# Adding up all three passes of a split product in one PSUM bank, and another order for the first operations

## The chip, the cores and the metric

The kernel runs on one core of a Trainium2 chip. The metric is the device time of one execution in microseconds (us), as the median of several runs. Beside it stands a profiled execution, from which all views are taken; its span runs from the first to the last instruction of the program.

Engines: PE is the matrix engine (PEld its weight loads), DVE the vector engine, ACT the scalar engine, POOL the general engine, SP the queue that issues DMAs. PE writes its sums to PSUM, which consists of banks of 512 float32 values for each of 128 partitions; ACT and DVE read them from there.

## The reference

A decayed linear attention over blocks of 64 tokens, then a two-layer network with a leaky ReLU on its output:

```python
q, k, v: (4, 8, 768, 64) float32     lam: (8,) float32
w_in: (512, 2048) float64            w_out: (2048, 512) float64
...
for b in range(nb):
    intra = (qb @ kb.T * Dmask) @ vb
    inter = (qb * lam_pow) @ kv_state
    out[b] = intra + inter
    kv_state = lam_block * kv_state + (kb * rev_pow).T @ vb
x = attn_out as (3072, 512)
h = x @ w_in
g = maximum(0.01 * h, h)
return float32(g @ w_out)
```

The weights come as 64-bit floats. The kernel turns each into float32 with integer and ACT arithmetic on its two words (`to_float32`).

## The kernel before

**Split products.** A float32 product is made from three passes of a faster format (`float32r`). An operand is split into a head `h`, a rest `l` and a combination `m`; a weight likewise into `wh`, `wl`, `wm` (`parts`, line 802). The passes are xh by wh (z = 0), xl by wl (z = 1) and xm by wm (z = 2). The first two have another scale than the third. So the sum of the first two is multiplied by S + 1 (S = 4096) before the third is added to it.

**Stages.** The 3072 tokens are 24 chunks of 128 (`NCH`), in six groups of four (`NG`, `GC`). Three stages overlap:

- *Attention rounds* (`round_of(c)`, one for each chunk). A round loads k, q and v (lines 466, 524), transposes k and q on PE (L546), copies them from PSUM to SBUF on ACT (L527), and makes scores, states and outputs from many small 64x64 products (L410). The output of a chunk arises in the PSUM tile `po`. ACT takes its head `xh` from there (L692), DVE its rest `xl` (L700), and then `xm` (L718). From chunk 4 on, the transposed k of a later chunk uses the upper half of the same tile `po`, and ACT copies it from there.
- *`up(g, p)`*, the first layer for group g and weight part p (of `NP` = 8). For each half of the part it takes a PSUM bank, adds passes 0 and 1 into it (4 products of 512 columns each), scales the bank in place on ACT (L878), adds pass 2, and applies the leaky ReLU on ACT (L881) into a buffer `gs`, which goes to DRAM as `G`.
- *`down(g, p)`*, the second layer. `down_load` brings G back and splits it (L902 on ACT, L903 and L905 on DVE) into a ring of four. For each of four row blocks (`tb`) of 128 tokens, all parts are added up: passes 0 and 1 in one bank, pass 2 in another. After the last part ACT takes the first bank with its scale to `t` (L943), DVE adds the second (L952), and the rows go out (L955). In the last block of all, pass 2 is cut into 384 and 128 columns, so that the first cut can be added while the second is still computed.

**Banks.** `psc` and `po` are PSUM tiles of two banks each; `pt`, `b10`, `b11` and `b2` have one each. In `up` and in the first rounds, blocks take any of the four single ones. In `down` the row blocks have fixed pairs:

```python
acc = [[z[:, i].rearrange("p y t -> p (y t)") for i in range(2)] for z in (psc, po)] + [
    [b1[0], b2], [b1[1], pt.rearrange("p y t -> p (y t)")]]
ACC = [["psc", "psc"], ["po", "po"], ["b10", "b2"], ["b11", "pt"]]
```

So row block 0 has both banks of psc, 1 both of po, 2 has b10 and b2, 3 has b11 and pt, in every group.

**Order.** A planner (`Plan`) records every operation by `add(engine, cost, function, reads, writes)`. A list `ORDER` gives the first operations by number, with the engine that takes each: (8, "ACT") is operation 8, on ACT. A negative number on PE is so many filler transposes (L349), which keep PE running; nine more (`WARM`) stand ahead of the list. What is not listed, the planner orders by costs and due times. Operations are emitted in that order, and each engine works its own in the order of emission. Waits between engines are put in when the program is built, from which tiles an instruction reads and writes. An engine that waits holds up everything behind it in its queue. SP's queue also counts DMAs on eight semaphores in turn.

Of the kernel before, what the change touches and what calls it, by code (L numbers as in the profile page):

```python
# [27 lines left out]
U = 16.0  # L28
WS = S * U

# [211 lines left out]
def kernel(  # L242
# [22 lines left out]
    T = GC * C  # L265
    WARM = 9
    LATER = 2.0
    ORDER = [(3, "DMA"), (4, "DMA"), (-6, "PE"), (6, "PE"), (8, "ACT"), (7, "PE"), (5, "DMA"), (9, "ACT"), (0, "DVE"), (1, "DVE"), (10, "POOL"), (13, "PE"), (2, "DVE"), (11, "DVE"), (15, "DVE"), (12, "PE"), (14, "DVE"), (-1, "PE"), (19, "PE"), (20, "PE"), (16, "POOL"), (17, "DVE"), (21, "DVE"), (101, "DMA"), (26, "DMA"), (29, "PE"), (33, "DVE"), (22, "PE"), (28, "DMA"), (36, "PE"), (18, "POOL"), (38, "DVE"), (39, "POOL"), (103, "ACT"), (23, "ACT"), (24, "DVE"), (27, "DMA"), (31, "ACT"), (102, "ACT"), (30, "PE"), (32, "ACT"), (-1, "PE"), (35, "PE"), (37, "DVE"), (40, "DVE"), (41, "POOL"), (34, "DVE"), (105, "DVE"), (49, "DMA"), (95, "DMA"), (96, "ACT"), (104, "ACT"), (52, "PE"), (56, "DVE"), (42, "PE"), (43, "PE"), (97, "ACT"), (50, "DMA"), (-1, "PE"), (53, "PE"), (98, "ACT"), (54, "ACT"), (55, "ACT"), (44, "DVE"), (25, "DVE"), (106, "DVE"), (99, "DVE"), (51, "DMA"), (-2, "PE"), (59, "PE"), (45, "PE"), (61, "DVE"), (100, "DVE"), (72, "DMA"), (73, "DMA"), (46, "ACT"), (75, "PE"), (107, "ACT"), (58, "PE"), (57, "DVE"), (47, "DVE"), (60, "DVE"), (76, "PE"), (155, "PE"), (74, "DMA"), (179, "DMA"), (78, "ACT"), (62, "POOL"), (79, "POOL"), (108, "DVE"), (63, "DVE"), (77, "ACT"), (173, "DMA"), (80, "DVE"), (48, "DVE"), (65, "PE"), (66, "PE"), (67, "ACT"), (-2, "PE"), (68, "PE"), (156, "PE"), (-1, "PE"), (81, "PE"), (180, "ACT"), (69, "ACT"), (70, "DVE"), (64, "POOL"), (84, "DVE"), (85, "POOL"), (181, "ACT"), (182, "ACT"), (174, "ACT"), (175, "ACT"), (82, "PE"), (83, "DVE"), (157, "PE"), (158, "PE"), (120, "DMA"), (111, "DMA"), (110, "DMA"), (119, "DMA"), (112, "DMA"), (88, "PE"), (89, "PE"), (114, "PE"), (159, "ACT"), (90, "ACT"), (91, "PE"), (176, "ACT"), (92, "ACT"), (183, "DVE"), (109, "DVE"), (160, "PE"), (123, "PE"), (86, "DVE"), (177, "DVE"), (184, "DVE"), (93, "DVE"), (178, "DVE"), (-1, "PE"), (164, "PE"), (113, "PE"), (165, "PE"), (161, "PE"), (217, "DMA"), (211, "DMA"), (136, "DMA"), (117, "DVE"), (116, "ACT"), (125, "ACT"), (115, "ACT"), (128, "PE"), (129, "PE"), (135, "DMA"), (121, "DMA"), (185, "ACT"), (71, "DVE"), (127, "DVE"), (186, "DVE"), (122, "PE"), (219, "ACT"), (124, "ACT"), (162, "ACT"), (166, "PE"), (241, "PE"), (167, "PE"), (242, "PE"), (138, "PE"), (87, "POOL"), (94, "DVE"), (118, "DVE"), (218, "ACT"), (213, "ACT"), (214, "ACT"), (212, "ACT"), (221, "DVE"), (131, "DVE"), (130, "DVE"), (-1, "PE"), (137, "PE"), (139, "PE"), (140, "PE"), (232, "DMA"), (132, "POOL"), (126, "DVE"), (133, "DVE"), (134, "POOL"), (220, "ACT"), (142, "PE"), (143, "PE"), (215, "DVE"), (222, "DVE"), (141, "ACT"), (243, "ACT"), (168, "ACT"), (144, "PE"), (145, "ACT"), (149, "ACT"), (148, "ACT"), (246, "PE"), (247, "PE"), (169, "PE"), (187, "DVE"), (216, "DVE"), (223, "ACT"), (244, "PE"), (170, "PE"), (234, "ACT"), (248, "ACT"), (151, "DVE"), (224, "DVE"), (153, "DVE"), (189, "DMA"), (226, "DMA"), (163, "DMA"), (188, "DMA"), (154, "DMA"), (275, "DMA"), (252, "PE"), (253, "PE"), (171, "ACT"), (233, "ACT"), (228, "ACT"), (227, "ACT"), (235, "ACT"), (249, "PE"), (191, "PE"), (152, "DVE"), (146, "DVE"), (190, "PE"), (150, "POOL"), (225, "DVE"), (229, "ACT"), (236, "DVE"), (230, "DVE"), (231, "DVE"), (192, "PE"), (193, "PE"), (194, "DVE"), (195, "PE"), (196, "PE"), (197, "PE"), (245, "ACT"), (202, "ACT"), (250, "ACT"), (237, "DVE"), (238, "DVE"), (206, "DVE"), (239, "DVE"), (254, "ACT"), (201, "ACT"), (277, "PE"), (320, "DMA"), (322, "ACT"), (288, "ACT"), (198, "ACT"), (321, "ACT"), (257, "PE"), (258, "PE"), (255, "PE"), (172, "DMA"), (326, "DMA"), (327, "ACT"), (204, "DVE"), (324, "DVE"), (207, "POOL"), (208, "DVE"), (203, "POOL"), (328, "ACT"), (259, "ACT"), (323, "ACT"), (330, "DVE"), (205, "DVE"), (199, "DVE"), (325, "DVE"), (329, "ACT"), (331, "DVE"), (332, "DVE"), (333, "DVE"), (268, "PE"), (269, "PE"), (263, "PE"), (256, "ACT"), (260, "PE"), (352, "DMA"), (274, "DMA"), (354, "ACT"), (210, "DMA"), (276, "PE"), (278, "PE"), (279, "PE"), (298, "DMA"), (281, "PE"), (282, "PE"), (355, "ACT"), (280, "ACT"), (261, "ACT"), (283, "PE"), (300, "PE"), (340, "PE"), (264, "PE"), (284, "ACT"), (311, "ACT"), (346, "DMA"), (251, "DMA"), (289, "POOL"), (209, "POOL"), (292, "DVE"), (293, "POOL"), (353, "ACT"), (265, "ACT"), (291, "DVE"), (446, "DVE"), (335, "PE"), (341, "PE"), (287, "ACT"), (348, "ACT"), (336, "PE"), (349, "ACT"), (270, "ACT"), (347, "ACT"), (356, "DVE"), (240, "DVE"), (266, "PE"), (267, "ACT"), (285, "DVE"), (271, "PE"), (272, "ACT"), (337, "ACT"), (296, "DMA"), (297, "DMA"), (299, "PE"), (301, "PE"), (302, "PE"), (303, "ACT"), (262, "DMA"), (411, "DMA"), (405, "DMA"), (294, "DVE"), (463, "DVE"), (334, "DVE"), (471, "DMA"), (458, "DMA"), (477, "DMA"), (455, "DMA"), (350, "DVE"), (357, "DVE"), (304, "PE"), (305, "PE"), (351, "DVE"), (306, "PE"), (338, "PE"), (358, "ACT"), (310, "ACT"), (307, "ACT"), (359, "DVE"), (308, "DVE"), (286, "DVE"), (309, "DVE"), (450, "DMA"), (273, "DMA"), (339, "ACT"), (342, "ACT"), (413, "ACT"), (407, "ACT"), (406, "ACT"), (388, "PE"), (361, "PE"), (343, "PE"), (362, "PE"), (344, "ACT"), (383, "PE"), (384, "PE"), (389, "PE"), (479, "DMA"), (454, "DMA"), (319, "DMA"), (470, "DMA"), (478, "DMA"), (447, "DMA"), (457, "DMA"), (366, "PE"), (367, "PE"), (360, "DVE"), (314, "DVE"), (200, "DVE"), (295, "POOL"), (412, "ACT"), (415, "DVE"), (147, "DVE"), (385, "ACT"), (390, "ACT"), (414, "ACT"), (408, "ACT"), (368, "ACT"), (391, "PE"), (386, "PE"), (369, "PE"), (468, "DMA"), (345, "DMA"), (472, "DMA"), (431, "DMA"), (437, "DMA"), (451, "DMA"), (464, "DMA"), (363, "ACT"), (364, "PE"), (365, "ACT"), (387, "ACT"), (370, "ACT"), (371, "DMA"), (459, "DMA"), (448, "DMA"), (449, "DMA"), (313, "POOL"), (290, "POOL"), (409, "DVE"), (315, "DVE"), (316, "POOL"), (317, "DVE"), (416, "DVE"), (494, "PE"), (495, "PE"), (312, "POOL"), (497, "PE"), (498, "PE"), (496, "DVE"), (499, "PE"), (410, "DVE"), (417, "DVE"), (461, "DMA"), (453, "DMA"), (462, "DMA"), (456, "DMA"), (503, "DVE"), (392, "ACT"), (452, "DMA"), (460, "DMA"), (393, "DMA"), (418, "DVE"), (432, "ACT"), (435, "DVE"), (433, "ACT"), (434, "ACT"), (436, "DVE"), (394, "PE"), (395, "PE"), (396, "ACT"), (439, "ACT"), (399, "PE"), (440, "ACT"), (372, "PE"), (425, "PE"), (373, "PE"), (438, "ACT"), (374, "ACT"), (465, "DMA"), (474, "DMA"), (400, "PE"), (401, "ACT"), (397, "PE"), (426, "PE"), (402, "PE"), (513, "DVE"), (441, "DVE"), (419, "DVE"), (442, "DVE"), (443, "DVE"), (510, "DVE"), (475, "DMA"), (398, "ACT"), (403, "ACT"), (512, "DMA"), (404, "DMA"), (480, "DVE"), (522, "DVE"), (377, "PE"), (375, "PE"), (376, "ACT"), (427, "ACT"), (555, "PE"), (378, "PE"), (379, "ACT"), (476, "DMA"), (469, "DMA"), (420, "PE"), (421, "PE"), (422, "ACT"), (380, "PE"), (556, "PE"), (381, "ACT"), (423, "PE"), (428, "PE"), (444, "DVE"), (467, "DMA"), (529, "DMA"), (473, "DMA"), (525, "DMA"), (561, "DMA"), (445, "DVE")]
    APART = 4
    FIRST_LOADS = ["k0", "q0", "v0", "k1", "q1", "v1", "w10", "k2", "q2", "v2", "w11", "k3", "q3", "v3"]  # L270
    LOW_PE, MIX_PE = set(), set()
# [772 lines left out]
```

## Time and profile before

| | us |
|---|---|
| median of 3 runs | 608.91 (608.42 to 609.12) |
| span of the profiled execution | 606.1 |
| PE busy, of the span | 595.4 |
| PE idle while waiting, all of it before 31 us | 7.5 |
| DVE / ACT / POOL busy | 308.5 / 266.9 / 73.4 |
| attention rounds and `up` on PE | to about 340 |
| `down` on PE | about 340 to 603 |
| last output row lands | 606.1 |

The busy times say that PE sets the time: in the 40 equal slices of the span every one but the first, second and last is at 9 tenths or more. A product of 512 columns starts 0.227 us after the one before (twelve take 2.72 us), though its own row is 389 ns long, because products are pipelined. An idle stretch of ACT or DVE costs nothing while PE has work.

### The profile page before, as it was taken

How to read it: one execution, taken by the hardware profiler on the slowest of the kernel's cores; microseconds unless marked ns; L12 is line 12 of the kernel's file. 1: busy time of each engine (PE TensorE's matmuls, PEld its weight loads, DVE VectorE, ACT ScalarE, POOL GpSimd, SP SyncE). 2: the span in 40 equal slices, each digit the busy share in tenths (PEclk: the TensorE clock that was granted, in tenths of full speed). 3: DMA queues.
4: the chain of work that ended last, by engine and by line, in shares of the span. 5: the costliest groups of instructions: out<-in, count | busy, mean ns of one | idle time of the engine just before them, and what ended most of it. 6: DMA issues, size and time to landing. Idle time of an engine off the chain costs nothing.

```text
span 606.1 us, 12896 instructions
## 1 busy us (share of the span) xinstructions
PE 595.4 (98%) x5381; PEld 494.4 (82%) x5381; DVE 308.5 (51%) x425; ACT 266.9 (44%) x428; POOL 73.4 (12%) x83
## 2 busy tenths in 40 slices
PE   7899999999999999999999999999999999999997
PEld 5688888888888888888788888888888888888886
DVE  5888855334242344243467755455454544635531
ACT  3789865444555556565566432222312313214111
POOL 2232412214132023122000000000000000000000
PEclk9999999999999999999999999999999999999999
DMA  8998957676889878975775833423333333333201
GB/s 194 230 260 226 267 164 215 148 183 153 202 247 216 215 240 191 262 246 176 263 277 213 290 122 115 163 83 143 122 108 135 109 135 113 132 104 122 87 1 69
DMA packets 147754, 105.18 MB, mean 174 GB/s; under 512 B 123632, under 2 KB 124400, under 8 KB 147696
## 3 DMA queue, kind: packets, MB, share of 16 engines
q1 hardware_dynamic: 147408, 104.29, 58.1%
q8 instruction: 42, 0.69, 0.5%
q14 instruction: 16, 0.13, 0.1%
q10 hardware_dynamic: 288, 0.07, 0.0%
HBM read 68.69 MB, written 35.65 MB: 172 GB/s over the span
## 4 chain that ended last, share of the span: by engine, by line
PE 96%; SPq 2%; DMA 1%; issue 0%; DVE 0%; DVEq 0%; ACT 0%
PE b L853 33%; PE b L920 18%; PE pt L853 11%; PE po L920 11%; PE psc L920 11%; PE po L410 4%; PE pt L920 4%; PE psc L410 3%; SPq L466 2%; DMA gs<-in_k_dram 1%; PE b L546 1%; PE po L546 0%; SPq L781 0%; SPq L524 0%; PE pt L546 0%
## 5 line engine op out<-in xcount | busy, mean ns | idle before, releaser
L902 ACT ACTIVATE xh<-att 128x1024 fp32r<-128x1024 f32 x48 | 50.7, 1060 | 148.7 <-PE b L920 140.7
L903 DVE SCALAR_TENSOR_TENSOR xl<-att,xh 128x1024 fp32r<-128x1024 f32 x48 | 58.6, 1222 | 97.7 <-ACT xh L902 97.7
L853 PE MATMUL b<-xm,wm 128*128 128x512 f32 (+1 forms) x292 | 77.6, 391 | 0.0
L853 PE MATMUL b<-xh,wh 128*128 128x512 f32 (+1 forms) x292 | 77.4, 389 | 0.0
L853 PE MATMUL b<-xl,wl 128*128 128x512 f32 (+1 forms) x292 | 77.4, 388 | 0.0
L920 PE MATMUL b<-wh,xh 128*128 128x512 f32 x192 | 74.7, 389 | 0.0
L920 PE MATMUL b<-wl,xl 128*128 128x512 f32 x192 | 74.7, 389 | 0.0
L853 PEld LDWEIGHTS b<-xl,wl 128*128 128x128 f32 x292 | 54.2, 188 | 11.2
L853 PEld LDWEIGHTS b<-xh,wh 128*128 128x128 f32 x292 | 54.0, 188 | 11.1
L853 PEld LDWEIGHTS b<-xm,wm 128*128 128x128 f32 x292 | 53.5, 188 | 11.4 <-ACT b L878 0.3
L905 DVE SCALAR_TENSOR_TENSOR xm<-xl,xh 128x1024 fp32r<-128x1024 f32 x48 | 58.7, 1226 | 4.7
L878 ACT ACTIVATE b<-b 128x512 f32<-128x512 f32 x72 | 42.0, 586 | 34.8 <-PE b L853 34.8
L881 ACT ACTIVATE gs<-b 128x512 f32<-128x512 f32 x72 | 42.6, 597 | 30.3 <-PE b L853 24.3
L920 PEld LDWEIGHTS b<-wl,xl 128*128 128x128 f32 x192 | 36.0, 188 | 7.5
L920 PEld LDWEIGHTS b<-wh,xh 128*128 128x128 f32 x192 | 36.1, 188 | 7.4
L647 POOL TENSOR_TENSOR att<-att 128x256 f32<-128x256 f32 x40 | 30.9, 772 | 86.8 <-DVE att L644 73.9
L637 DVE TENSOR_TENSOR att<-psc,att 128x512 f32<-128x512 f32 x24 | 16.5, 689 | 45.4 <-PE psc L410 45.3
L920 PE MATMUL psc<-wm,xm 128*128 128x512 f32 (+1 forms) x100 | 37.9, 384 | 0.0
L799 DVE TENSOR_SCALAR w<-w 128x512 int32<-128x512 int32 x32 | 14.9, 468 | 44.1 <-ACT w L793 44.0
L920 PE MATMUL psc<-wh,xh 128*128 128x512 f32 x96 | 37.3, 389 | 0.0
L920 PE MATMUL psc<-wl,xl 128*128 128x512 f32 x96 | 37.3, 389 | 0.0
L920 PE MATMUL po<-wh,xh 128*128 128x512 f32 x96 | 37.3, 389 | 0.0
(98 smaller groups left out, 944.4 us busy)
## 6 DMA issues: line engine op xcount, KB each, us to landing
att<-g SPq DMA_DIRECT2D x48, 512.0 KB, 3.2
g<-gs SPq DMA_DIRECT2D x47, 512.0 KB, 3.6
raw<-in_moe_w_in_dram SPq DMA_DIRECT2D x16, 512.0 KB, 5.3
raw<-in_moe_w_out_dram SPq DMA_DIRECT2D x16, 512.0 KB, 4.6
out_dram<-gs SPq DMA_DIRECT2D x23, 256.0 KB, 2.1
att<-in_k_dram SPq DMA_DIRECT2D x44, 128.0 KB, 4.1
att<-in_v_dram SPq DMA_DIRECT2D x22, 256.0 KB, 4.1
wo<-w SPq DMA_DIRECT2D x8, 512.0 KB, 4.9
```

The source lines that it names most:

```text
L410: nc.tensor.matmul(dst[HALF[cols]], lhsT=lhsT[HALF[rows]], rhs=rhs[HALF[rows]], start=start, stop=True, skip_group_check=True)
L466: nc.sync.dma_start(out=dst[:, z * HP:(z + 1) * HP, :], in_=y[z::2].rearrange("h p d -> p h d"))
L637: add("DVE", 0.685, lambda: nc.vector.tensor_tensor(sc, psc[:, :, lower, :], decay, op=ALU.mult), ["psc", "fk"], ["sc"])
L647: add("POOL", 0.62, lambda new=new, j=j: nc.gpsimd.tensor_tensor(state[(j + 1) % 4], new, _bc(lam_c, 2, D), op=ALU.mult), [f"st{j % 4}", " ...
L799: add("DVE", 0.42, lambda: nc.vector.tensor_scalar(d, d, 3, None, op0=ALU.logical_shift_left), [], [key], lock=True)
L853: nc.tensor.matmul(dst, lhsT=w[z][:, kk * 2 * P + f * P:kk * 2 * P + (f + 1) * P], rhs=x[z][:, kk, toks], start=start and kk == 0, stop=kk ...
L878: add("ACT", ns, lambda b=b: nc.scalar.activation(out=b(), in_=b(), func=AF.Copy, bias=0.0, scale=S + 1.0), [], [kb], rank=-1.5)
L881: add("ACT", ns, lambda b=b, r=r: nc.scalar.activation(out=r(), in_=b(), func=AF.Prelu, bias=0.0, scale=1.0 / WS, alpha=0.01), [kb], [kg], ...
L902: add("ACT", 1.05, lambda: nc.scalar.activation(out=h, in_=graw[j], func=AF.Copy, bias=0.0, scale=NEAR), reads, wr("h"))
L903: add("DVE", 1.215, lambda: nc.vector.scalar_tensor_tensor(l, graw[j], 1.0, h.bitcast(F32), op0=ALU.mult, op1=ALU.subtract), reads + [f"rh ...
L905: add("DVE", 1.215, lambda: nc.vector.scalar_tensor_tensor(m, l.bitcast(F32), -S, h.bitcast(F32), op0=ALU.mult, op1=ALU.add), [f"rh{j}", f ...
L920: nc.tensor.matmul((to if z == 2 else acc[tb][0])[:, cols], lhsT=ring[j][z][:, f * T + tb * P:f * T + (tb + 1) * P], rhs=W[pp][z][:, f * d ...
```

## The change

**`up`.** All three passes of a half add up in one bank with no scaling between; the leaky ReLU follows with scale 1.

```diff
             for i, f in enumerate(fs):
                 add("PE", us, lambda f=f, b=b, i=i: product(b()[:, i, :], f, 0, i == 0), keys("h"), [kb], kind="u")
                 add("PE", us, lambda f=f, b=b, i=i: product(b()[:, i, :], f, 1), keys("l"), [kb], kind="u")
             ns = 0.6 if len(fs) * n == T else 0.4
-            add("ACT", ns, lambda b=b: nc.scalar.activation(out=b(), in_=b(), func=AF.Copy, bias=0.0, scale=S + 1.0), [], [kb], rank=-1.5)
             for i, f in enumerate(fs):
                 add("PE", us, lambda f=f, b=b, i=i: product(b()[:, i, :], f, 2), keys("m"), [kb], kind="u")
-            add("ACT", ns, lambda b=b, r=r: nc.scalar.activation(out=r(), in_=b(), func=AF.Prelu, bias=0.0, scale=1.0 / WS, alpha=0.01),
+            add("ACT", ns, lambda b=b, r=r: nc.scalar.activation(out=r(), in_=b(), func=AF.Prelu, bias=0.0, scale=1.0, alpha=0.01),
                 [kb], [kg], rank=-1.5)
```

**Weight parts.** For that, the scale goes into the second part: the head is a plain copy, `wm` = w - wh, and `wl` = (S + 1) wm + wh. The order of `wl` and `wm` is exchanged. The conversion's scale changes from 2^-110 to 2^-112.

```diff
-                nc.scalar.activation(out=wh, in_=src, func=AF.Copy, bias=0.0, scale=NEAR / S)
+                nc.scalar.copy(wh, src)
...
-        add("DVE", 1.215, lambda: nc.vector.scalar_tensor_tensor(wl, wh.bitcast(F32), -S, src, op0=ALU.mult, op1=ALU.add),
-            keys + [f"wh{p}"], [f"wl{p}"], lock=True)
-        difference(p)
...
+        add("DVE", 1.215, lambda: nc.vector.scalar_tensor_tensor(wm, wh.bitcast(F32), -1.0, src, op0=ALU.mult, op1=ALU.add),
+            keys + [f"wh{p}"], [f"wm{p}"], lock=True)
+        add("DVE", 1.215, lambda: nc.vector.scalar_tensor_tensor(wl, wm.bitcast(F32), S + 1.0, wh.bitcast(F32), op0=ALU.mult, op1=ALU.add),
+            [f"wh{p}", f"wm{p}"], [f"wl{p}"], lock=True)
```

**`down`.** A row block has one bank. The eight banks make two sets: row blocks of even groups use psc's two banks and po's two, those of odd groups use b10, b2, b11 and pt. The planner knows the halves of psc and po by names of their own. A finished block is copied by ACT straight into the output buffer, with no `t` and no sum on DVE. Only the last block of all keeps `t` and the two sums; its third pass goes to two banks of the other set, the halves of psc.

```diff
-    acc = [[z[:, i].rearrange("p y t -> p (y t)") for i in range(2)] for z in (psc, po)] + [
-        [b1[0], b2], [b1[1], pt.rearrange("p y t -> p (y t)")]]
-    ACC = [["psc", "psc"], ["po", "po"], ["b10", "b2"], ["b11", "pt"]]
+    acc = [z[:, i].rearrange("p y t -> p (y t)") for z in (psc, po) for i in range(2)] + [b1[0], b2, b1[1], bank["pt"]]
+    ACC = ["psc0", "psc1", "po0", "po1", "b10", "b2", "b11", "pt"]
...
+            at = g % 2 * GC + tb
...
+            spare = [(1 - g % 2) * GC + i for i in range(2)]
...
+                if not very_last:
+                    add("ACT", 0.6, lambda y=y, at=at: nc.scalar.copy(y, acc[at]), [ACC[at]], [f"gs{jt}"], rank=-1.5)
+                    add("DMA", 0.8, lambda rows=rows, y=y: nc.sync.dma_start(out=rows, in_=y), [f"gs{jt}"], [], rank=-1.5)
+                    continue
...
-                        lambda t=t, y=y, to=to, cols=cols: nc.vector.scalar_tensor_tensor(
-                            y[:, cols], to[:, cols], 1.0 / WS, t[:, cols], op0=ALU.mult, op1=ALU.add),
+                        lambda t=t, y=y, to=to, cols=cols: nc.vector.tensor_tensor(y[:, cols], acc[to][:, cols], t[:, cols], op=ALU.add),
```

**`ORDER`.** The list is another one: 364 operations and 6 fillers where it had 491 and 16. Operations are renumbered, since `up` records fewer. It begins with one half of weight part 1 (95), then q and k of chunk 0 (4, 3), k of chunk 1 (26), v of chunk 0 (5), q of chunk 1 (27), the other half (101) and v of chunk 1 (28). Before, it began with k, q and v of chunk 0 (3, 4, 5), the half 101, then k, v and q of chunk 1 (26, 28, 27), k of chunk 2 (49) and the half 95. Each k and each q is two DMAs, so half 101 was the sixth load. In round 7 of the new list the head `xh` of the output is operation 276, the rest `xl` 277, and the copy of kT for chunk 9 is 279. On ACT and DVE the list has, from the one to the other:

```python
(276, "ACT"), (321, "ACT"), (284, "DVE"), (198, "DVE"), (316, "DVE"), (317, "DVE"), (255, "ACT"),
(279, "ACT"), (283, "DVE"), (322, "DVE"), (323, "DVE"), (324, "DVE"), (277, "DVE")
```

More of the change, by code (lines that the diff above doesn't have):

```diff
@@ L27 @@
 NEAR = 1.0 - 2.0 ** -13
-U = 16.0
-WS = S * U
 def _bc(ap, idx, n):
@@ L355 @@
     kinds = {"bank": list(bank), "raw": [f"raw{i}" for i in range(NRAW)], "low": ["low0", "low1"], "gs": ["gs0", "gs1"]}
-    also = {"gs0": ["gs00", "gs01", "k@2", "v@2"], "gs1": ["gs10", "gs11", "k@3", "v@3"], f"raw{NRAW - 1}": [f"raw{NRAW - 1}", "q@3"]}
+    also = {"gs0": ["gs00", "gs01", "k@2", "v@2"], "gs1": ["gs10", "gs11", "k@3", "v@3"], f"raw{NRAW - 1}": [f"raw{NRAW - 1}", "q@3"], "psc": ["psc0", "psc1"], "po": ["po0", "po1"]}
     early = [Slot("gs", 0), Slot("gs", 1), Slot("raw", NRAW - 1)]
@@ L792, in to_float32 @@
         move(1.6, get, after, [kr], name=f"w{p}{h}" if kind == "wi" else None)
-        add("ACT", 0.66, lambda: nc.scalar.activation(out=dst, in_=words(1, F32), func=AF.Abs, scale=2.0 ** -110),
+        add("ACT", 0.66, lambda: nc.scalar.activation(out=dst, in_=words(1, F32), func=AF.Abs, scale=2.0 ** -112),
             [kr], [key])
@@ L919, in go @@
                         for z in zs:
-                            nc.tensor.matmul((to if z == 2 else acc[tb][0])[:, cols], lhsT=ring[j][z][:, f * T + tb * P:f * T + (tb + 1) * P],
+                            nc.tensor.matmul(to[:, cols], lhsT=ring[j][z][:, f * T + tb * P:f * T + (tb + 1) * P],
                                              rhs=W[pp][z][:, f * d_model:(f + 1) * d_model][:, cols],
-                                             start=pp == 0 and f == 0 and z != 1, stop=pp == NP - 1 and f == 1,
+                                             start=fresh and pp == pps[0] and f == 0 and z == zs[0], stop=pp == NP - 1 and f == 1,
                                              skip_group_check=True)
@@ L930, in down @@
             cut = [slice(0, 3 * P), slice(3 * P, d_model)]
-            ends = [(acc[tb][1], ACC[tb][1]), (acc[0][1], ACC[0][1])]
+            spare = [(1 - g % 2) * GC + i for i in range(2)]
             one, two = (p,), (p + 1,)
-            order = [(one, (0, 1, 2), every), (two, (0, 1, 2), every)]
+            order = [(one, (0, 1, 2), every, at), (two, (0, 1, 2), every, at)]
             if very_last:
-                order = [(one + two, (0, 1), every)] + [(one + two, (2,), x) for x in cut]
-            for pps, zs, cols in order:
-                to, key = ends[cut.index(cols)] if cols in cut else (acc[tb][1], ACC[tb][1])
-                add("PE", 0.227 * 2 * len(pps) * len(zs) * (cols.stop - cols.start) / d_model, lambda pps=pps, zs=zs, cols=cols, to=to, go=go: go(pps, zs, cols, to),
-                    needs(pps, ["hlm"[z] for z in zs]), sorted({key if z == 2 else ACC[tb][0] for z in zs}))
+                order = [(one + two, (0, 1), every, at)] + [(one + two, (2,), x, y) for x, y in zip(cut, spare)]
+            for pps, zs, cols, to in order:
+                fresh = to in spare or 0 in pps
+                add("PE", 0.227 * 2 * len(pps) * len(zs) * (cols.stop - cols.start) / d_model,
+                    lambda pps=pps, zs=zs, cols=cols, to=to, go=go, fresh=fresh: go(pps, zs, cols, acc[to], fresh),
+                    needs(pps, ["hlm"[z] for z in zs]), [ACC[to]])
             if done:
@@ L942, in down @@
                 t, y = tt[jt], gs[jt][:, 0, :]
-                add("ACT", 0.6, lambda t=t, tb=tb: nc.scalar.activation(out=t, in_=acc[tb][0], func=AF.Copy, bias=0.0, scale=(1.0 + 1.0 / S) / U),
-                    [ACC[tb][0]], [f"t{jt}"], rank=-1.5)
                 rows = out[(g * GC + tb) * P:(g * GC + tb + 1) * P, :]
-                for i, cols in enumerate(cut if very_last else [every]):
+                if not very_last:
+                    add("ACT", 0.6, lambda y=y, at=at: nc.scalar.copy(y, acc[at]), [ACC[at]], [f"gs{jt}"], rank=-1.5)
+                    add("DMA", 0.8, lambda rows=rows, y=y: nc.sync.dma_start(out=rows, in_=y), [f"gs{jt}"], [], rank=-1.5)
+                    continue
+                add("ACT", 0.6, lambda t=t, at=at: nc.scalar.copy(t, acc[at]), [ACC[at]], [f"t{jt}"], rank=-1.5)
+                for i, cols in enumerate(cut):
                     n = cols.stop - cols.start
-                    to, key = ends[i]
-                    part_of = f"gs{jt}" + (str(i) if very_last else "")
-                    queue = nc.scalar if i else nc.sync
+                    to, part_of, queue = spare[i], f"gs{jt}{i}", nc.scalar if i else nc.sync
                     add("DVE", 0.14 + 0.55 * n / d_model,
-                        lambda t=t, y=y, to=to, cols=cols: nc.vector.scalar_tensor_tensor(
-                            y[:, cols], to[:, cols], 1.0 / WS, t[:, cols], op0=ALU.mult, op1=ALU.add),
-                        [f"t{jt}", key], [part_of], rank=-1.5)
+                        lambda t=t, y=y, to=to, cols=cols: nc.vector.tensor_tensor(y[:, cols], acc[to][:, cols], t[:, cols], op=ALU.add),
+                        [f"t{jt}", ACC[to]], [part_of], rank=-1.5)
                     add("DMA", 0.8 * n / d_model, lambda rows=rows, y=y, cols=cols, queue=queue: queue.dma_start(out=rows[:, cols], in_=y[:, cols]),
```

10 lines of the change are left out of this document (3 added, 7 removed).

## The prediction

> **What bounds the kernel now.** I read the page's busy shares first, then the busy time by stretch, then TensorE's own waits.
>
> ```profile
> PE 595.4 (98%) x5381; PEld 494.4 (82%) x5381; DVE 308.5 (51%) x425; ACT 266.9 (44%) x428; POOL 73.4 (12%) x83
> ...
> PEclk9999999999999999999999999999999999999999
> ```
> ```profile
> 0.00:45.00 45.00, 37.84 (x819) 32.21 (x820) 33.99 (x70) 29.49 (x50) 13.06 (x20) 1.00 0.94 228
> 45.00:340.00 295.00, 294.72 (x3402) 244.44 (x3402) 145.21 (x236) 173.52 (x307) 60.31 (x63) 1.00 0.77 218
> 340.00:602.00 262.00, 262.00 (x1158) 217.06 (x1157) 128.58 (x118) 63.45 (x73) 0.00 (x0) 1.00 0.33 115
> ```
> ```profile
> PE b L349 <- POOL att L352: 1.4, 1, 1.4
> PE b L546 <- DMA gs<-in_k_dram: 1.3, 1, 1.3
> PE b L410 <- DMA att<-in_v_dram: 1.1, 1, 1.1
> ...
> PE psc L410 <- ACT att L527: 0.6, 1, 0.6
> ```
> In the second view the columns are the stretch, its length and the busy time of PE, PEld, DVE, ACT and POOL, then clock, DMA share and GB/s. From 45 to 602 us PE is busy 556.7 of 557.0 us, at full clock. All of PE's waits together are 7.5 us, in the head, while the first loads land. So work that leaves ACT or DVE after 45 us is worth nothing; the change can win only in the head, and it can lose wherever it puts a wait on PE.
>
> **What it removes.** The products stay: six token groups x 8 parts x 48 of 512 columns, 2304 in all at one every 0.227 us (the chain has 12 in 2.72 us), 523 us. The scaling in the middle of each `up` block goes:
> ```profile
> L878 ACT ACTIVATE b<-b 128x512 f32<-128x512 f32 x72 | 42.0, 586 | 34.8 <-PE b L853 34.8
> ...
> L878 ACT ACTIVATE pt<-pt 128x512 f32<-128x512 f32 x24 | 14.0, 583 | 17.9 <-PE pt L853 17.9
> ...
> L943 ACT ACTIVATE raw<-po 128x512 f32<-128x512 f32 x6 | 3.6, 598 | 12.7 <-PE po L920 12.7
> ...
> L527 ACT COPY att<-po 128x512 f32<-128x512 f32 x6 | 3.6, 592 | 1.1 <-PE po L546 0.9
> ```
> That is 56.0 us of ACT, plus 23 additions of 0.69 on DVE (L952) in `down`. All of it but the share in the head lies under a busy PE: 0. The reworked weight parts are as many instructions of the same shapes, so I cost them as the old rows: 0. If these covers went, nothing follows: both engines are under 60% busy there.
>
> **Down banks: +5.6.** Until now the four row blocks of a group used psc, po, the pair b/b2 and the pair b/pt, so a tile that ACT was emptying was not written again until three blocks later. Now blocks 0 and 1 of an even group are the two halves of psc, and 2 and 3 those of po. In the built program the last pair's first product into psc's second half waits for ACT's copy out of the first half, and the same in po: twice a group, groups 0, 2 and 4, six waits. Odd groups use four separate tiles and have none. One wait: the block's last product ends 0.39 after its start (L920's mean is 389 ns), ACT starts 0.03 later (at the end PE finishes po at 597.23, L943 starts at 597.26), the copy takes 0.59 (L527 on po, above), PE restarts 0.05 later (an L527 ending at 14.54 released PE at 14.60). That is 1.06, less the 0.227 that PE would have spent anyway, 0.83. Then a first product whose weights could not be loaded ahead:
> ```profile
> 41.47 1.20 PE L853 MATMUL b<-xh,wh 128*128 128x512 f32 x4
> 42.51 1.08 PE L853 MATMUL b<-xl,wl 128*128 128x512 f32 x4
> ```
> The first four after other work take 0.12 more; I use 0.11. 6 x 0.94 = 5.6. Bounds: 4.8 with the shortest copy (557 ns) and no reload; 12 if ACT has each time just begun a ring head of 1.06 (L902). ACT is 24% busy here and took the block 0.03 after PE, so the value is near the lower end.
>
> **Round 7's split: +4.4.** In the new list `xh` of round 7 is (276, "ACT"), `xl` (277, "DVE"), and between them stands (279, "ACT"), the copy of kT for a later round. All three read po. In the built program `xl` waits for that copy, which is eighth after `xh` in ACT's queue: six weight operations (L795, L797, L793) and a block's end (L881) are in between. Start to start, ACT takes less than the durations:
> ```profile
> 64.08 0.80 ACT L795 ACTIVATE low<-raw 128x512 uint16<-128x512 uint32 x1
> 64.73 0.79 ACT L797 ACTIVATE low<-raw 128x512 f16<-128x512 f32 x1
> ...
> 70.16 0.59 ACT L527 COPY att<-po 128x512 f32<-128x512 f32 x1
> 70.64 0.60 ACT L692 ACTIVATE xh<-po 128x512 fp32r<-128x512 f32 x1
> ```
> Here 0.65 for L795; likewise 0.63 for L797, 0.55 for L793 and 0.50 for L881. In the queue: 0.50 for `xh`, then 0.65 + 0.50 + 0.63 + 0.55 + 0.65 + 0.63 + 0.55 = 4.16, then the copy's 0.59: 5.25. Then DVE's 0.68 and two hand-overs of 0.05: 6.0, and 0.25 from the last attention product to `xh`: 6.25. PE has eight products queued ahead, 8 x 0.227 + 0.13 to change over = 1.95. So PE stands 4.3, near 70 us, and 0.11 for weights: 4.4. Before, the copy stood ahead of `xh` (70.16, 70.64), and `xl` came right behind at 71.28. Bounds: 0 if `xl` waited for `xh` alone (ready 1.4 after it starts, under the 1.95); 7.4 if two of the weights' loads, which ACT also waits for in that queue, land 1.5 late. Behind `xl` on DVE stand only `xm` and state sums for the same round.
>
> **Round 11: +1.2.** Group 2's first product follows the attention products of round 11 at once and needs their `xh`: 0.25 + 0.60 + 0.05 = 0.9, and then `xl` (0.68 + 0.1) against four products (0.91) that began late, 0.2, with 0.1 for weights. Before, 24 products of blocks with other operands stood there (139.01 to 145.46). Bounds 0 and 2.
>
> **End: +0.3.** The last block's third pass goes into psc's two halves, not pt and psc, so DVE's first sum waits for the second cut:
> ```profile
> 602.31 0.56 PE L920 MATMUL psc<-wm,xm 128*128 128x128 f32 x4
> 602.56 0.56 DVE L952 SCALAR_TENSOR_TENSOR gs<-pt,raw 128x384 f32<-128x384 f32 x1 [1.48 <-PE pt L920]
> ```
> It starts after 602.87 instead of 602.56. Bounds 0 and 0.4.
>
> **Head: -1.3.** The list drops ten filler transposes (25 L349 rows to 15), 10 x 0.11 = 1.1 where they weren't in a wait, and halves the changes between transposes and attention products, 26 to 13 at about 0.1: 1.3. Against it, SP issues a 512 KB weight half first: that load landed 1.58 after the one ahead of it (9.04 after 7.46), so q0 and k0 come about 1.6 later; k1, which moves up past v0, comes 1.8 earlier (v0's own 7.46 less 5.70), and q1 and the second half, past v1, 1.2 earlier (11.28 less 10.13). The first round is late by 1.6 and the later ones are early, so I take 1.1 more waiting. Bounds: -6 (all waits but the first gone) and +3 (the late start never made up).
>
> Sum: 5.6 + 4.4 + 1.2 + 0.3 - 1.3 = +10.2. The profiled execution's span is 606.1 us; the median of the runs, 608.9, lies 2.8 above it; I carry that over. So 616.3 for the span and **619.1 us**.
>
> **Rivals.**
> (a) The wait in `down` goes by bank, not by tile: then the 5.6 and the 0.3 vanish, 613.2. For it: PE fills one half of psc while the other is read, nothing collides. Against: the built program's waits. [...]
> (b) `xl` isn't held by the copy: 4.4 less, 614.7. For it: both only read po. Against: the wait is in the program.
> (c) After standing 4.3 us, longer than any wait of before (1.4), PE restarts slowly, as it started: warm-up transposes took 417 ns, later ones 272. At double interval for some 4.4 us that costs 2.2: 621.3. Against: full clock in every slice after waits of 1.4. [...]
> (d) Faster: the head fills sooner. The scalings in the first 45 us leave ACT, which is 29.5 us busy there, and loads come in the order of need. All PE waits but the first are 6.1, with 1.3 of fillers and changes 7.4 at most; it decides only if the stalls of (a) and (b) are not there either: 0.3 to 1.2 left, 602.7 to 607.
>
> **How the numbers follow.** Forecast 70% (615.5 to 622), (a) 6%, (b) 6%, (c) 10%, (d) 6%, no change 2%. The likeliest gives 619.1. The range 613.0 to 622.5 takes in (a), (b) and (c) and most of the head's bounds, and leaves out (d). Under 0.2% (1.2 us) can't be told from no change here: faster 6%, same 2%, slower 92%.
>
> **What would show it.** Six PE waits of 0.8 to 0.9 on ACT near 380, 387, 470, 477, 560 and 567 us, none in odd groups; one PE wait of 4 to 5 us near 70 us on DVE; about 1 us near 143; the rest of PE's waits before 45 us, 7 to 9 us in all. Total PE waits near 18 us. Wrong if PE stays gapless after 45 us, or if the head's waits fall under 3 us.

## The result and the profile after

The changed kernel takes 628.14 us (median of 4 runs, 627.01 to 629.56); the kernel before took 609.00 beside it (608.42 to 609.12). The ratio is 1.0322, 95% interval 1.0301 to 1.0343. The change is slower by 19.1 us; 619.1 had been forecast, a loss of 10.2, and the range ended at 622.5. The profiled execution took 629.56, 627.8 of it span, against 606.1 before; it is the slowest of the four, so the two traces lie further apart than the medians. Of the ten executions each of three_mended and three_and_head below, one took far longer at a much lower granted clock (852.52 us at 0.658 and 667.5 at 0.851), and the medians given there leave it out.

The same three views, now of the changed kernel. First the page's shares and the clock by slice:

```profile
PE 602.2 (96%) x5371; PEld 496.3 (79%) x5371; DVE 294.6 (47%) x401; ACT 213.5 (34%) x330; POOL 75.0 (12%) x86
...
PEclk8999999999998999999999999999999999999999
```

ACT lost 53.4 us of work, and the end came 21.7 later. Two slices of the clock, the first and the thirteenth, are below full speed; before there was none. The stretches up to 45 us, to 340 and to the last product:

```profile
0.00:45.00 45.00, 37.04 (x809) 31.04 (x810) 33.71 (x69) 25.65 (x43) 14.81 (x23) 0.96 0.95 231
45.00:340.00 295.00, 285.25 (x3335) 235.40 (x3334) 134.17 (x227) 117.43 (x206) 60.18 (x63) 0.98 0.73 204
340.00:623.90 283.90, 279.72 (x1231) 229.86 (x1229) 126.01 (x105) 70.39 (x81) 0.00 (x0) 1.00 0.35 121
```

From 45 to 340 us PE now stands 9.75 us, where it had stood 0.3, and after 340 another 4.2; the clock, third from the end of a line, is 0.98 in the middle stretch. PE's waits by what they waited for (total, times, longest):

```profile
PE b L848 <- DVE xl L698: 4.0, 1, 4.0
PE psc L408 <- DVE att L516: 2.4, 1, 2.4
PE po L914 <- ACT gs L940: 2.2, 3, 0.7
PE psc L914 <- ACT gs L940: 2.0, 3, 0.7
...
PE psc L408 <- issue: 1.5, 1, 1.5
...
PE b L848 <- ACT xh L690: 1.0, 1, 1.0
```

The first, third, fourth and last are the waits of the forecast: one on `xl` at 75.5 us, six on the copies in `down`, one on `xh` at 149.8. The second and the fifth were in no term of the sum. To see what each cost, I matched the two traces by the work that PE had started (each product by its steady interval: 0.227 us for 512 columns, 0.117 for 256, 0.0155 for a 64x64 quadrant) and took the lead of the one over the other:

| stretch of the changed trace | us later than before | what stands there |
|---|---|---|
| to 45 us | 0.2 | the head |
| 45 to 68 | 1.0 | part of a wait without releaser, 1.5 at 69.0 |
| 68 to 80 | 6.8 | rest of that, the stand on `xl`, half clock |
| 80 to 155 | 1.0 | the wait on `xh` after round 11 |
| 155 to 200 | 6.2 | the stand on `att` (L516), half clock |
| 200 to 340 | 0.1 | |
| 340 to 600 | 5.9 | six waits in `down` |
| to the end | 0.5 | |
| sum | 21.7 | 627.8 - 606.1 |

**The clock.** In stretches of 3.41 us around the two large stands (columns as above: PE, PEld, DVE, ACT, POOL busy, clock, DMA share, GB/s):

```profile
72.69:76.10 3.41, 0.55 (x2) 0.48 (x3) 1.26 (x2) 2.08 (x4) 0.00 (x0) 1.00 0.79 199
76.10:79.51 3.41, 3.41 (x9) 2.63 (x8) 3.41 (x7) 0.00 (x0) 1.58 (x2) 0.50 0.96 290
79.51:82.93 3.42, 3.42 (x16) 2.82 (x15) 3.32 (x5) 0.80 (x1) 0.96 (x1) 1.00 0.06 15
...
181.91:185.33 3.42, 1.18 (x80) 1.04 (x72) 1.22 (x3) 1.56 (x3) 0.00 (x0) 1.00 1.03 294
185.33:188.74 3.41, 2.65 (x50) 2.24 (x51) 3.23 (x8) 1.43 (x3) 1.97 (x2) 0.50 0.81 189
188.74:192.15 3.41, 3.41 (x9) 2.64 (x9) 3.27 (x6) 0.00 (x0) 1.85 (x4) 0.50 0.71 274
192.15:195.57 3.42, 3.42 (x16) 2.81 (x16) 0.00 (x0) 0.60 (x1) 0.95 (x1) 1.00 0.37 93
```

PE is "busy" throughout 76.10 to 79.51, but issues 9 products where the next stretch has 16. The stretch before it holds 0.55 us of work. With one more of 3.41 at 7.83 in the head, the clock was halved for 13.65 us, at most 6.8 us of full-speed work. The busy column alone would have hidden this: a product at half clock counts as busy.

**The stand near 75 us** is the one described, on the right instructions:

```profile
69.63 0.60 ACT L690 ACTIVATE xh<-po 128x512 fp32r<-128x512 f32 x1 [5.63 <-PE po L408]
...
74.19 0.59 ACT L525 COPY att<-po 128x512 f32<-128x512 f32 x1
...
74.80 0.69 DVE L698 TENSOR_TENSOR xl<-po,xh 128x512 fp32r<-128x512 f32 x1 [4.72 <-ACT att L525]
...
75.55 1.62 PE L848 MATMUL b<-xl,wl 128*128 128x512 f32 x4 [3.95 <-DVE xl L698]
```

`xh` to copy is 4.56 us on ACT (4.66 had been added up), and `xl` starts when the copy ends. The text before the result names wrong entries for it, though: 276, 277 and 279 are round 6's. Round 7's are `xh` 299, `xl` 300 and the copy of kT for chunk 9 302, with seven other operations of ACT between 299 and 302, the seven that the sum adds up; `xl` stands behind 302 in the list.

**The stand near 185 us**, SyncE's and DVE's rows of the changed kernel:

```profile
178.94 0.41 SPq L782 DMA_DIRECT2D raw<-in_moe_w_out_dram  x1
...
179.87 0.47 SPq L507 DMA_DIRECT2D att<-in_q_dram  x1
...
184.11 0.77 DVE L516 STREAM_TRANSPOSE att<-raw 128x256 f32<-128x256 f32 x2 [9.40 <-DMA att<-in_q_dram]
...
185.53 1.13 PE L408 MATMUL psc<-att 64*64 64x64 f32 x32 [2.44 <-DVE att L516]
```

Chunks 15 to 17 get k and q by 32 loads of 48 KB each that DVE then turns. The last of them is issued at 179.87, 0.9 after 512 KB of w_out, and lands at 184.10, 4.2 later. In the profile of before the load of w_out came behind the last part, and the part landed 3.1 after its issue:

```profile
168.89 0.47 SPq L509 DMA_DIRECT2D att<-in_q_dram  x1
169.46 0.41 SPq L784 DMA_DIRECT2D raw<-in_moe_w_out_dram  x1
```

There the turning began at 172.04 and PE's products of that round ran through at 172.40: just in time.

### The profile page after: what moved, and what is told of

Same layout as the page of the kernel before. It is cut to its first block, busy times and chain, and to the rows that moved or that the text cites. A ratio compares the mean times of both kernels' runs of the same rounds, so it can differ in the third digit from the quotient of the medians.

```text
span 627.8 us, 12734 instructions
## 1 busy us (share of the span) xinstructions
PE 602.2 (96%) x5371; PEld 496.3 (79%) x5371; DVE 294.6 (47%) x401; ACT 213.5 (34%) x330; POOL 75.0 (12%) x86
## 4 chain that ended last, share of the span: by engine, by line
PE 86%; SPq 5%; issue 2%; DMA 2%; DVE 2%; ACT 2%; POOL 0%; DVEq 0%; ACTq 0%; POOLq 0%
PE b L848 28%; PE b L914 16%; PE psc L914 11%; PE po L914 11%; PE pt L848 9%; PE pt L914 5%; PE po L408 3%; PE psc L408 2%; SPq L464 2%; SPq L507 2%; DMA gs<-in_k_dram 1%; DMA g<-gs 1%; DMA att<-in_q_dram 1%; ACT gs L940 1%; SPq L522 1%
## 5 line engine op out<-in xcount | busy, mean ns | idle before, releaser
L848 PE MATMUL b<-xl,wl 128*128 128x512 f32 (+1 forms) x300 | 81.3, 394 | 4.0 <-DVE xl L698 4.0
L848 PE MATMUL b<-xh,wh 128*128 128x512 f32 (+1 forms) x300 | 81.8, 395 | 1.0 <-ACT xh L690 1.0
L914 PE MATMUL b<-wh,xh 128*128 128x512 f32 x144 | 56.0, 389 | 0.0
L914 PE MATMUL b<-wl,xl 128*128 128x512 f32 x144 | 56.0, 389 | 0.0
L914 PE MATMUL b<-wm,xm 128*128 128x512 f32 x144 | 56.0, 389 | 0.0
L797 DVE TENSOR_SCALAR w<-w 128x512 int32<-128x512 int32 x32 | 18.5, 580 | 50.2 <-ACT w L791 50.2
L914 PE MATMUL psc<-wm,xm 128*128 128x512 f32 (+2 forms) x104 | 38.6, 382 | 0.0
L914 PE MATMUL po<-wm,xm 128*128 128x512 f32 x96 | 37.4, 389 | 0.0
L914 PE MATMUL po<-wl,xl 128*128 128x512 f32 x96 | 37.4, 389 | 0.0
L645 POOL TENSOR_TENSOR att<-att 128x256 f32<-128x256 f32 x40 | 28.5, 712 | 52.1 <-DVE att L642 46.3
```

What stands on the lines that cost most here:

```text
L645: add("POOL", 0.62, lambda new=new, j=j: nc.gpsimd.tensor_tensor(state[(j + 1) % 4], new, _bc(lam_c, 2, D), op=ALU.mult), [f"st{j % 4}", " ...
L797: add("DVE", 0.42, lambda: nc.vector.tensor_scalar(d, d, 3, None, op0=ALU.logical_shift_left), [], [key], lock=True)
L848: nc.tensor.matmul(dst, lhsT=w[z][:, kk * 2 * P + f * P:kk * 2 * P + (f + 1) * P], rhs=x[z][:, kk, toks], start=start and kk == 0, stop=kk ...
L914: nc.tensor.matmul(to[:, cols], lhsT=ring[j][z][:, f * T + tb * P:f * T + (tb + 1) * P], rhs=W[pp][z][:, f * d_model:(f + 1) * d_model][:, ...
```

## The experiments

"Excess" is a kernel's median less that of the kernel before in the same runs (608.4 to 610.3 by chip and hour). The changed kernel's is 19.1.

| kernel | us | excess | ratio, 95% interval |
|---|---|---|---|
| xl_first | 620.77 | 12.4 | 1.0189, 1.0143 to 1.0234 |
| banks_alternate | 622.32 | 13.9 | 1.0207, 1.0163 to 1.0252 |
| fill_the_stand | 622.76 | 14.4 | 1.0217, 1.0179 to 1.0255 |
| subs_first | 622.93 | 13.0 | 1.0215, 1.0190 to 1.0239 |
| three_mended | 611.72 | 1.8 | 1.0026, 1.0010 to 1.0043 |
| three_and_head | 612.14 | 2.2 | 1.0033, 1.0015 to 1.0051 |
| old_order_mended | 620.99 | 11.0 | 1.0186, 1.0158 to 1.0213 |
| old_order_two_mended | 610.33 | 1.2 | 1.0022, 1.0004 to 1.0040 |
| before_parts_first | 609.36 | 0.3 | 1.0008, 0.9989 to 1.0027 |
| fill_12 | 626.29 | 16.0 | 1.0257, 1.0142 to 1.0373 |
| fill_18 | 626.97 | 16.6 | 1.0268, 1.0143 to 1.0394 |

### xl_first: the split of round 7 without the copy in front

```diff
 ORDER = [...
-(302, "ACT"), (446, "DMA"), (445, "DMA"), (306, "DVE"), (300, "DVE"), (352, "PE"),
+(300, "DVE"), (302, "ACT"), (446, "DMA"), (445, "DMA"), (306, "DVE"), (352, "PE"),
```

> The changed kernel with one entry of the order moved: the rest xl of round 7 (operation 300, DVE) now stands ahead of the copy of kT (302, ACT) instead of behind it, so it need not wait for that copy. Theory (a wait, then a slow restart): PE's stand of 3.95 us near 75 us goes, and with it the half-clock stretch of 3.4 us behind it, worth 1.7; the stand near 185 us (2.44 and 0.57) shrinks or goes too if it was carried on from here, with its 6.8 us of half clock, worth 3.4. So 628.1 - 4.1 - 1.7 = 622.3 if only the first goes, 616 if the one at 185 goes as well. Rival 1 (the wait alone; half clock has another cause): 624.0, and the clock still drops near 76. Rival 2 (xl was never held by the copy): nothing changes, 628.

620.77: 6.7 of the excess went. In its profile (span 616.8) the wait on `xl` is gone, the clock is at full from the first record, 12.9 us, to the last product, and near 178 only one wait of 1.0 is left. Two of the four runs were at clock 1.0 (618.6 and 618.9), two at 0.992 (622.6 and 622.8). So the theory holds for the stand near 75 and its half clock (5.8 expected for the two); rival 2, no hold by the copy, falls. Rival 1 falls with fill_the_stand. The median lies between two groups of runs, so the 6.7 is rough. PE's wait for the turned parts near 180 us is absent from this trace, 1.69 in that of banks_alternate and 2.44 in the changed kernel's; that it comes and goes between the runs of one kernel too is likely, but the two slower runs have no trace.

### banks_alternate: the accumulators in another order

```diff
-    acc = [z[:, i]... for z in (psc, po) for i in range(2)] + [b1[0], b2, b1[1], bank["pt"]]
-    ACC = ["psc0", "psc1", "po0", "po1", "b10", "b2", "b11", "pt"]
+    acc = [z[:, i]... for i in range(2) for z in (psc, po)] + [b1[0], b2, b1[1], bank["pt"]]
+    ACC = ["psc0", "po0", "psc1", "po1", "b10", "b2", "b11", "pt"]
```

> The changed kernel with the down product's accumulators in the order psc first half, po first half, psc second half, po second half, so that two row blocks that follow one another never share a tile, and the last block's third pass ends in psc and po. Theory (six waits of 0.95 us by tile, and 0.3 at the end): the six PE waits near 394, 401, 483, 490, 572 and 579 us go, 628.1 - 5.7 - 0.3 = 622.1. Rival (the waits move to the next block, or ACT's copy is late there too): they stay as waits of 0.3 to 0.7 elsewhere in the even groups, 625 to 628. Half clock near 76 and 185 us is untouched by this in both.

The excess fell by 5.2. After 340 us no PE wait is left in its trace, and matched by work it loses nothing there (36.6 us behind steady work at 340 and 36.5 at 600; the changed kernel 40.9 and 46.7). The median is rough here too, since its four runs lie between clock 0.997 and 0.986. One line of the changed kernel shows a wait and what follows:

```profile
393.14 0.39 PE L914 MATMUL psc<-wm,xm 128*128 128x512 f32 x1
394.20 0.50 PE L914 MATMUL psc<-wh,xh 128*128 128x512 f32 x1 [0.68 <-ACT gs L940]
394.54 0.39 PE L914 MATMUL psc<-wl,xl 128*128 128x512 f32 x1
```

Start to start 1.06 and 0.34 instead of 0.227 and 0.227: 0.94, the value of the forecast. The idle 0.68 that the row names is only part of it, because the product before has a modelled end.

### fill_the_stand, fill_18, fill_12: PE busy, but no earlier

```diff
-(300, "DVE"), (352, "PE"),
+(300, "DVE"), (-36, "PE"), (352, "PE"),
```

> The changed kernel with 36 transposes of the identity (about 4 us) put into the order on PE just ahead of the product that waits for xl of round 7: PE waits as long for its data, but is not idle. They write nothing that is used. Theory (half clock follows from an idle PE): the half-clock stretch near 76 us is gone, the start of the products after it is as late as before, 628.1 - 1.7 = 626.4; the stretch near 185 us stays, since its stand stays. Rival 1 (half clock has another cause, such as the load of all engines): it stays near 76, 628. Rival 2 (the transposes delay the products): slower than 628.

In its profile there is no half clock near 76, as the theory has it: transposes that serve nothing save time. The excess fell by 4.7, more than the 1.7 of that stretch. By work matched, 0.9 less was lost to 45 us, 2.1 less from there to 80 and 1.9 less from 155 to 200, where one stretch of half clock came in place of two. Only what went near 75 us is the edit's doing; in the rest the two traces differ by chance. The wait ahead of the same products is unmoved. fill_18 and fill_12 have 18 and 12 in place of 36:

> As fill_the_stand with 12 transposes (1.3 us) in place of 36, so PE stands some 2.6 us idle near 75 us, where the changed kernel stood 3.95. In the traces so far half clock came in stretches of 3.41 us, on a grid of that length: where PE had been idle 2.2 us or more of one such window (of 3.41) the next was at half clock, after 1.7 it wasn't. Theory (it goes by the idle share of the window before): half clock behind the stand if over 2.2 of the 2.6 fall into one window, none if they are split 1.3 and 1.3; the windows are read off the trace. Rival (any stand over some length, wherever it lies): half clock as with 3.95. Time 622 to 627, the rest as the changed kernel.

> As fill_12 with 18 transposes (2.0 us): PE stands some 2.0 us idle near 75 us. Theory (idle share of the window before): no half clock there unless all of it falls into one window, and then it tells the bound between 1.7 and 2.2. Rival (any stand): half clock. Time 622 to 626.

PE stood 2.65 us in fill_12 and 2.01 in fill_18, and half clock followed both. In fill_18, by windows of the grid that its half-clock stretch gives:

```profile
70.23:73.64 3.41, 3.28 (x24) 2.69 (x22) 0.00 (x0) 3.41 (x7) 1.32 (x2) 1.00 0.67 193
73.64:77.06 3.42, 1.54 (x7) 1.28 (x8) 2.25 (x5) 1.10 (x3) 0.00 (x0) 1.00 0.79 193
77.06:80.47 3.41, 3.41 (x10) 2.67 (x9) 3.41 (x6) 0.42 (x1) 2.54 (x2) 0.50 0.77 204
```

Idle 1.88 of the middle window was enough. It wasn't in banks_alternate near 180, with 1.69:

```profile
180.13:183.55 3.42, 1.73 (x86) 1.35 (x88) 1.51 (x4) 1.83 (x4) 0.06 (x1) 1.00 0.91 265
183.55:186.96 3.41, 2.41 (x54) 1.98 (x55) 3.41 (x8) 1.15 (x3) 2.43 (x2) 1.00 0.89 193
```

Here a wait of 1.69 and one of 1.00 fell into two windows, and the clock stayed. Within one execution all half-clock stretches begin a whole number of 3.41 us apart (7.83, 76.10 and 185.33 in the changed kernel: 20 and 32 windows). So it goes by the idle share of a fixed window; the rival, any stand over some length, isn't excluded for stands over 2 us, since each of those also filled over half of one window. In the head the bound is less clear: half clock once followed a window with 1.27 idle (before_parts_first, 13.7 us) and once one with 1.69 (fill_18, 8.8 us), but the ends of the short products there are modelled.

### subs_first: the parts for chunks 15 to 17 ahead of w_out

`RUNS` has the rank of the first of these loads and the step from one to the next; what isn't named has 4.0 and 0.4. A lower rank goes first, and the planner takes 0.0 here as -8.0, the rank of its other loads (`FIRST`).

```diff
-    RUNS = {10: (-8.0, 0.8), 12: (4.0, 0.0)}
+    RUNS = {10: (-8.0, 0.8), 12: (4.0, 0.0), 15: (0.0, 0.0)}
```

> The changed kernel with the loads of q and k in parts for chunks 15 to 17 (L507) ranked earlier, so that SP issues the last of them ahead of a load of w_out (L782) and not 0.9 us behind it. Theory (the stand near 185 us is the last of these loads landing late, at 184.1, 4.2 after its issue, behind 512 KB of w_out that landed at 183.75): the stand of 2.44 + 0.57 goes, and with it 6.8 us of half clock, worth 3.4: 628.1 - 6 = 622; the stand near 75 stays. Rival 1 (the whole queue of SP is late, and one place in it helps little): the stand shrinks by under 1 and half clock stays near 185: 626 to 628. Rival 2 (the load of w_out that is now later stops ACT and then PE): a new wait on ACT after 190 us, 625 to 630.

The excess fell by 6.1. SyncE now issues the last three parts at 173.04 to 175.98 and w_out after them:

```profile
173.04 2.94 SPq L507 DMA_DIRECT2D att<-in_q_dram  x3
...
177.70 0.53 SPq L782 DMA_DIRECT2D raw<-in_moe_w_out_dram  x1
178.08 1.30 DVE L516 STREAM_TRANSPOSE att<-att 128x512 f32<-128x512 f32 x2 [3.92 <-DMA att<-in_k_dram]
...
182.75 1.11 PE L408 MATMUL psc<-att 64*64 64x64 f32 x64
```

The 64 products that had stood 2.44 run through, and there is no half clock after 79 us. A wait of 0.89 on `seen_po` (L674) at 184.75 is left. Both rivals fall. The last part is now issued over 7 us ahead of the products that need it (175.51 for some 183.2), where the changed kernel had some 3; so the run shows that the parts were late, and not how much of that came from their place behind w_out.

### three_mended and three_and_head

> The changed kernel with the three edits together: xl of round 7 ahead of the copy of kT, accumulators alternating, the parts for chunks 15 to 17 earlier. Theory (the stands and the half clock behind them are the loss): 3.95 + 0.1 and 1.7 near 75, 3.0 and 3.4 near 185, 5.7 and 0.3 in down: 628.1 - 18.2 = 610, with the waits near 149 (1.0) and in the head left; clock 0.997 or more. Rival (the loss moves to the next late load): 613 to 618, with a PE wait of over 1 us on DVE or ACT between 150 and 300.

The three edits together leave 1.8 of the 19.1; alone they took 6.7, 5.2 and 6.1, together 18.0 and in one kernel 17.3. They are nearly independent. Its longest waits:

```profile
PE pt L544 <- DMA att<-in_q_dram: 1.8, 1, 1.8
PE psc L408 <- issue: 1.7, 1, 1.7
PE pt L544 <- issue: 1.6, 1, 1.6
PE b L347 <- POOL att L350: 1.4, 1, 1.4
PE b L848 <- ACT xh L690: 0.8, 1, 0.8
```

> As three_mended, with 14 transposes of the identity instead of 6 behind the nine that warm PE up, so that PE isn't idle until q of chunk 0 lands at 6.6 us. They write nothing that is used. Theory (half clock from 7.8 to 11.2 us follows from PE standing 1.96 at 4.7 to 6.6): full clock from 7 us on, as before the change, and 0.5 to 1.7 less than three_mended. Rival (the head waits for loads anyway): the same as three_mended within 0.5, with the waits behind 12 us longer.

```diff
-(-6, "PE"),
+(-14, "PE"),
```

612.14 against 611.72: the rival holds, the waits in the head were only filled. The first record of full clock is at 4.6 us in this profile and at 13.7 in that of three_mended, and it made nothing.

### The old order with the new arithmetic

> The changed kernel's arithmetic and banks with the order of the kernel before, its operations renumbered, the scalings left out, and wm and wl of each weight part where wl stood. This tells what the new arithmetic and banks cost without the new order. Theory 1 (the order costs all but the down waits): 609.0 + 5.7 + 0.3 = 615. Theory 2 (wl now needs wm first, two operations of 1.2 us on DVE, and the old order asks PE for wl too early): waits of 1 to 5 us on DVE in the first 140 us, with half clock behind the long ones, 625 to 640.

This kernel computes something else: two of the operations in each weight part were taken from `w_out`'s, and its 649.47 us tells nothing of the question. With the numbers mended:

> The changed kernel's arithmetic and banks with the order of the kernel before, renumbered; wm and wl of each w_in part stand where wl stood. In old_order the renumbering had put the parts of w_out in the place of those of w_in, so that products read parts that were not yet written and it tells nothing. Theory 1 (arithmetic costs nothing, the order brings the stand near 75): 609.0 + 5.7 + 0.3 = 615, no half clock near 75. Theory 2 (the arithmetic itself costs time in the first 140 us, since wl comes 1.2 later on DVE): waits on DVE before 60 us, 617 to 620.

620.99, so theory 1 (615) falls, and not for theory 2's reason alone: the six waits are there, nothing stands near 75 us, but at 178.1 PE waits 2.1 for the turned parts and at 179.8 another 1.0 for a copy behind them on DVE (L674), with half clock behind. There, too, SyncE issues w_out at 172.26, ahead of the last part at 172.72. So this stand isn't the new list's doing. Then both defects mended at once, with the old order:

```diff
-    RUNS = {10: (-8.0, 0.8), 12: (4.0, 0.0)}
+    RUNS = {10: (-8.0, 0.8), 12: (4.0, 0.0), 15: (2.0, 0.2)}
...
-    ACC = ["psc0", "psc1", "po0", "po1", "b10", "b2", "b11", "pt"]
+    ACC = ["psc0", "po0", "psc1", "po1", "b10", "b2", "b11", "pt"]
```

> The arithmetic of the changed kernel with the order of before (as old_order_mended), the accumulators alternating and the parts for chunks 15 to 17 ranked 2.0 + 0.2 instead of 4.0 + 0.4. Theory (the six waits, and the late parts with their half clock, are no matter of the order): 621.0 - 5.8 - 3.1 - 1.7 = 610.4, that is within 0.3% of before; left are the waits for wl before 50 us, about 1. Rival 1 (the arithmetic gains once its defects are gone): under 608. Rival 2 (the parts are late in this order whatever their rank): 613 to 616, with a stand near 175 us.

610.33, as expected (610.4), 1.2 over before. The waits on `wl` (24.9 and 47.5 us, 0.7 and 0.3) are left: `wl` is now made from `wm`, one operation later on DVE. Rival 1, a gain once the defects are gone, falls.

### before_parts_first

> The kernel before with only the rank of the parts for chunks 15 to 17 changed, 2.0 + 0.2 instead of 4.0 + 0.4. Most of its runs on this chip show a clock of 0.997 or less and 609.5 to 612, those at 1.0 lie at 607.6 to 609.5. Theory (before, too, stands at times near 173 us for these parts, which came 0.8 us ahead of their need in its profile): runs at 1.0 become the rule, 608.3 where before has 610, ratio 0.997. Rival (the lost window of before lies elsewhere): the same time as before, ratio 0.999 to 1.001.

No difference (0.9989 to 1.0027): a miss. In this profile the one window at half clock lies at 13.7 us, in the head; where the other runs of the kernel before lose theirs is not shown. No version run here beats the kernel before.

## Why the prediction was wrong

From the 10.2 of the sum to the 21.7 of the traces, 6.2 are the loss near 185 us, 1.7 the half clock near 76, some 1.6 the wait near 68, 1.5 the head, and 0.5 the small misses of the other terms. The number looks better than that by luck: the forecast carried over 2.8 from the span to the median, and here it was 0.3.

**What bounds the kernel, and the removed work: right.** 56 us of ACT were worth nothing, and the mended kernels, which have all of that saving, end 1.2 and 1.8 us above before. They show it as well as a run can: nothing gained on ACT came to PE.

**Down banks (+5.6): right.** Six waits, none in odd groups, 0.94 each; 5.9 in the trace, and 5.2 of the median came back with alternating banks (which holds the end's share too). Rival (a), a wait by bank, falls: the waits were there, as the built program had them. They are the program's waits; no run shows whether the chip needs them.

**Round 7's split (+4.4): the wait right, its consequence not.** PE stood 3.95 by its row, some 4.2 with the modelled end and the weights. Rival (b) falls with xl_first. The step that failed is the one that gave (c) 10%: "PE restarts slowly" happened, and the argument against it, full clock in every slice after waits of 1.4, was a comparison with waits that fill less than half of a window. It cost 1.7 here, near the 2.2 that (c) had. A window idle in part was enough to bring it on: 2.24 of 3.41 in the changed kernel (181.91), 1.88 in fill_18 (73.64), so a stand of 2.01 had it behind it too. (c) had estimated double interval for 4.4 us; behind this stand it was one window of 3.41, with 9 products where the next had 16.

**The sum had no term between 143 and 340 us.** That is the other failed step, and the larger: 6.2 us. The change was followed through ACT, DVE and PE, but SyncE's order of loads was looked at in the head only. From 150 to 180 us it issues nearly without a pause, half a microsecond each, and one load of 512 KB changed places with two parts that were just in time before. The rows name 3.0 of stand (2.44 and 0.57), and two windows of half clock are up to 3.4, less what of the stand lies in them; together 6.2 by the work matched.

**Round 11 (+1.2): a size.** The wait is there at 149.8, 1.04; 1.0 in the stretch that holds it. **End (+0.3):** 0.4, from the start of the last product to the end 3.94 instead of 3.55. **Head (-1.3): wrong by 1.5.** The late start was made up, as forecast (8.7 us behind steady work at 10 us against 7.7 before, 13.0 against 12.9 at 20), but not more than that. The fillers and changes taken away bought nothing, because PE then waits for loads (1.96 on q0 at 6.65 and 1.38 on a k at 22.54 in the changed kernel's trace): three_and_head. Against that, the head before held 0.85 of a wait that now comes at 68 us instead (below).

**Not settled.** What in the planner puts w_out ahead of the last parts with the new arithmetic is open; that ACT is free earlier, so that its load is due earlier, is only argued.

The wait near 68 us stands in the middle of 64 products of one operation, with no releaser in any trace. All kernels with the new list have it, 0.4 to 1.7 long. It isn't new with that list: the kernel before and all with the old list have one like it at 26 to 28 us, 0.2 to 1.7 long.

```profile
27.27 0.56 PE L410 MATMUL psc<-att 64*64 64x64 f32 x20 [0.85 <-issue]
...
68.98 0.35 PE L408 MATMUL psc<-att 64*64 64x64 f32 x9 [1.47 <-issue]
```

In every trace the wait stands ahead of the same instruction: 962 rows of PE (weight loads, products, semaphores) come before it with the old list and 2,498 with the new, which is 6 x 256 more. And in every trace a load of 16 KB on the queue that the profile calls instruction begins 2.2 to 2.8 us before the wait ends (at 24.83 and at 66.66 in the two above); an execution has 42 of these loads, about one for each 256 of PE's rows. So PE seems to stand for its own instructions there, in a place that the order of the list decides. No run tests this.

## What to carry to other kernels

When PE is full, price a stand of about 2 us or more with the half clock behind it: here 1.7 us for a window of 3.41, and twice that where the restart has waits of its own. Follow every queue that the change or a planner reorders to the end of the program, the DMA queue first: a load that was just in time has no margin, and the busy shares don't show it. To see half clock, count products in equal stretches; the busy time doesn't tell.

## What the runs showed of the hardware

Half clock came only in whole windows of 3.41 us on one grid through an execution. After 45 us, it always began behind a window in which PE was idle for 1.88 us or more (fill_18), never behind one with 1.69 or less (banks_alternate), and 36 transposes in the stand kept it away (fill_the_stand: 0.06 idle from 72.92 to 76.33, clock 1.00 behind). It went on there for a second window where the first had 0.77 idle (185.33 in the changed kernel), and ended after one with 0.16 (182.16 in fill_the_stand) or less; in the head of fill_12 it went on after one with 0.15 (7.62). Whether a stand of 2 to 3 us costs its clock depends on how the grid cuts it: 2.24 and 0.77 in two windows did (the changed kernel), 1.69 and 1.00 did not (banks_alternate). The runs of one kernel differ in it too, such as fill_18's, 628.45 at clock 0.992 and 625.48 at 1.0; that the cause is the phase of the grid is not shown, as only one run of each kernel has a trace.
